# Making the next pair's factors: loads one step ahead and in program order, T1 formed in the chunks, T2 to T4 formed from it on VectorE

## The chip, the cores and the metric

One core of one Trainium2 chip runs the whole program. The metric is the device time of one execution, in microseconds (us).

## The reference, cut to what matters

```
attn = windowed causal attention(q, k, v)        # 4 x 8 heads x 576 x 64, window 128, f32
x    = attn as (2304 tokens, 512)
x2   = (s * relu(x @ moe_w_in)**2 + b) @ moe_w_out        # 512 -> 2048 -> 512
a, b = x2 @ moe2_w1, x2 @ moe2_w2                         # 512 -> 1024 each
out  = ((a * b) @ moe2_w3) @ moe2_w_out                   # 1024 -> 1024 -> 512
```

All of it is float32. The change lies in the last two lines alone.

## The kernel before, in words

The 2304 tokens are six tiles of 384. Attention and the first network run tile by tile and leave x2, transposed, in DRAM (`x2d`), as four blocks of 128 features for each tile. Then `moe2_w3 @ moe2_w_out` is multiplied out once (`w3_unit`, line 601), so that the second network is two matrix products with an elementwise product between them.

These two products run over three **pairs** of token tiles, q = 0, 1, 2. Both are done as a seven-product scheme on two by two blocks (Strassen and Winograd): the blocks B11, B12, B21, B22 of the moving operand are turned into seven **factors**, B11, B21, T1, T2, T4, B22, T3, with T1 = B12 - B11, T2 = B22 - T1, T4 = T2 - B21, T3 = B22 - B12. Every factor is held as a high part (a rounded copy, made by ScalarE) and a low part (the difference, made by a subtraction); `split_to`, lines 652 to 654, does that. A product of two factors is then three passes of matmuls.

A pair has two stages.

**The chunk stage.** `pair_chunk` (line 913) runs for c = 0 to 7. Each chunk has seven products of six matmuls of 128x384 (`prod`, line 886), in the order A11, A12, S1, S2, A22, S4, S3 on TensorE, which is fixed by program order. Four PSUM tiles u, d, e, f take them, in one set of four banks for even chunks and the other for odd ones. ScalarE copies e, u and f out of PSUM (line 901) because the same banks are accumulated on again: S4 adds onto e, so its first matmul waits for the copy of e, which goes into one of two buffers tagged "r" and so waits for the readers of the chunk before. VectorE adds and multiplies (lines 922, 931, 933 to 935), and GpSimd does the last product, p2 (line 936). The results are `prods[c] = (p1, p2)`.

After the fourth product of each chunk but the last, `step` takes one step of `x_later(q + 1)`, which prepares the factors of the next pair: it loads x2 blocks into six buffers tagged "t" (line 796), forms the differences on VectorE (line 815), splits them (line 654) and stores both parts to DRAM (lines 811, 812). In the first pair `step` also takes a step of `w3_factors`, which splits the blocks of the multiplied-out weights with GpSimd for the low parts.

After each odd chunk `w_fetch` (line 754) fetches three weight tiles of 512 KB for the odd chunk two further on. `keep_in_program_order` ties an instruction behind the one that stands before it in the program on the same engine or queue. Instructions without it are placed by a planner that simulates the program's time. In `w_fetch` the three DMAs are tied, in `x_later` only the ScalarE copies are.

**The output stage.** `out_pair` (line 938) takes the eight `prods` as blocks: i = 0 to 3 give B11 and B12, i = 4 to 7 give B21 and B22. `factors` forms and splits the seven factors, four tiles each, into the eight "x" buffers; `product` (line 961) runs 24 matmuls for each, in the order B11 (u), B21 (d), T1 (e), T2 (u), T4 (f), B22 (e), T3 (u). T1, T2 and T4 are formed on VectorE (lines 948, 950, 952), T3 on GpSimd (line 954). `x_fetch` (line 843) fetches the next pair's factors: B11, B21 and T1 before the stage, T2 during it, and T4, B22 and T3 at its end, into the "x" buffers that the output's own factors leave. The results are stored by line 977, some of them from "t" buffers.

All DMAs of this part are issued by one queue, SP's.

Of the kernel before, what the change touches and what calls it, by code (L numbers as in the profile page):

```python
# [8 lines left out]
F32 = mybir.dt.float32  # L9
F32R = mybir.dt.float32r  # L10
# [3 lines left out]
ALU = mybir.AluOpType  # L14
# [13 lines left out]
NC2 = DF2 // P  # L28
# [12 lines left out]
def kernel(  # L41
# [607 lines left out]
        free_w[0] -= 1  # L649
        return wp.tile([P, 2, DM], F32R, tag="w", name="wblk")  # L650

    def split_to(dst, src, eng, pin=lambda i: i, lo_pin=None):
        pin(nc.scalar.activation(out=dst[0], in_=src, func=AF.Copy))  # L653
        (lo_pin or pin)(eng.tensor_tensor(out=dst[1], in0=src, in1=dst[0].bitcast(F32), op=ALU.subtract))  # L654

    wraw, lo_eng = {}, [nc.vector]

# [114 lines left out]
    def x2_at(q, nm, k):  # L772
        return x2d[2 * q + (nm[1] == "2")][k + 2 * (nm[0] == "2")]
# [15 lines left out]
    def x_later(q):  # L789


        def load(k, *nms):
            got[:] = []
            for nm in nms:
                r = lp.tile([P, TT], F32, tag="t", name="xs", bufs=6)
                nc.sync.dma_start(out=r, in_=x2_at(q, nm, k))
                got.append(r)

        def store(k, **rs):
            for nm, r in rs.items():  # L800
                if nz[0] % 3 == 2:
                    z = lp.tile([P, DM], F32, tag="z3", name="xh", bufs=1)[:, :TT]
                else:
                    z = zp.tile([P, TT], F32, tag="z", name="xh")
                nz[0] += 1
                split_to(
                    (z.bitcast(F32R), r.bitcast(F32R)), r, nc.vector,
                    tc.keep_in_program_order, lambda i: i,
                )
                d = xfd[q, nm, k]  # L810
                nc.sync.dma_start(out=d[:, 0, :], in_=z)
                nc.sync.dma_start(out=d[:, 1, :], in_=r)

        def sub(out, a, b):
            nc.vector.tensor_tensor(out=out, in0=a, in1=b, op=ALU.subtract)

        got = []
        load(0, "11", "21")
        yield
        for k in range(2):  # L820
            r11, r21 = got
            store(k, B11=r11, B21=r21)
            load(k, "11", "12", "22", "21")
            yield
            r11, r12, r22, r21 = got
            sub(r12, r12, r11)
            sub(r22, r22, r12)
            sub(r21, r22, r21)
            store(k, T1=r12, T2=r22)
            load(k, "22", "12")  # L830
            yield
            r22, r12 = got
            sub(r12, r22, r12)
            store(k, T4=r21, B22=r22, T3=r12)
            if k == 0:
                load(1, "11", "21")
            yield

    def x_fetch(q, names):
# [70 lines left out]
            t = wp.tile([P, 2 * DM], F32, tag="w", name="p")  # L910
        return [t[:, :TT], t[:, TT:2 * TT]]

    def pair_chunk(c, step):

        tt = nc.vector.tensor_tensor
        pool, tag = (ps_acc, "acc") if c % 2 else (ps_rot, "rot")
        u, d, e, f = (pool.tile([P, TT], F32, tag=tag, name=k) for k in ("u", "d", "e", "f"))
        prods[c] = p1, p2 = p_tiles(c)
        prod(u, "A11", "B11", c, True)
        keep_copy(u, y=p1)  # L920
        prod(d, "A12", "B21", c, True)
        tt(out=p1, in0=d, in1=p1, op=ALU.add)
        prod(e, "S1", "T1", c, True)
        m5 = keep_copy(e, gp, "r")
        prod(u, "S2", "T2", c, False)
        keep_copy(u, y=p2)
        step()
        prod(f, "A22", "T4", c, True)
        m4 = keep_copy(f, gp, "r")
        prod(e, "S4", "B22", c, False)  # L930
        tt(out=p2, in0=e, in1=p2, op=ALU.add)
        prod(u, "S3", "T3", c, False)
        tt(out=m4, in0=u, in1=m4, op=ALU.subtract)
        tt(out=p1, in0=p1, in1=m4, op=ALU.mult)
        tt(out=m5, in0=u, in1=m5, op=ALU.add)  # L935
        nc.gpsimd.tensor_tensor(out=p2, in0=p2, in1=m5, op=ALU.mult)  # L936

    def out_pair(q, before, after):

        tt = nc.vector.tensor_tensor  # L940
        n = NC2 // 2

        def factors(nm):
            ys = []
            for i in range(n):
                (b11, b12), (b21, b22) = prods[i], prods[i + n]
                if nm == "T1":
                    tt(out=b11, in0=b12, in1=b11, op=ALU.subtract)
                elif nm == "T2":
                    tt(out=b11, in0=b22, in1=b11, op=ALU.subtract)  # L950
                elif nm == "T4":
                    tt(out=b21, in0=b11, in1=b21, op=ALU.subtract)
                elif nm == "T3":
                    nc.gpsimd.tensor_tensor(out=b12, in0=b22, in1=b12, op=ALU.subtract)
                src = {"B21": b21, "T4": b21, "B22": b22, "T3": b12}.get(nm, b11)
                y = xp.tile([P, 2, TT], F32R, tag="x", name="pf")
                split_to((y[:, 0, :], y[:, 1, :]), src, nc.vector)
                ys.append(y)
            return ys

        def product(dst, wn, ys, start, outer=False):
            loops = [(i, m) for i in range(n) for m in range(2)]
            if outer:
                loops.sort(key=lambda x: x[1])
            for i, m in loops:
                w, off = w3f[wn, i]
                ms = slice(off + m * P, off + (m + 1) * P)
                for k, (l, r) in enumerate(PASSES):
                    tc.keep_in_program_order(nc.tensor.matmul(  # L969
                        out=dst[m], lhsT=w[:, l, ms], rhs=ys[i][:, r, :],  # L970
                        start=(start and i == 0 and k == 0), stop=(i == n - 1 and k == 2),
                        skip_group_check=True,
                    ))

        def store(z, half, m, t):
            r0 = (2 * half + m) * P
            nc.sync.dma_start(out=out[r0:r0 + P, t * TT:(t + 1) * TT], in_=z)

        d = [ps_rot.tile([P, TT], F32, tag="rot", name="od") for _ in range(2)]
        u = [ps_rot.tile([P, TT], F32, tag="rot", name="ou") for _ in range(2)]  # L980
        e = [ps_acc.tile([P, TT], F32, tag="acc", name="oe") for _ in range(2)]
        f = [ps_acc.tile([P, TT], F32, tag="acc", name="of") for _ in range(2)]
        y = factors("B11")
        before()
        y2 = factors("B21")
        product(u, "A11", y, True)
        m1 = [keep_copy(x, gp, "r") for x in u]
        y = factors("T1")
        product(d, "A12", y2, True)
        for m in range(2):  # L990
            tt(out=m1[m], in0=d[m], in1=m1[m], op=ALU.add)
            store(m1[m], 0, m, 2 * q)
        y2 = factors("T2")
        product(e, "S1", y, True)
        m5 = [keep_copy(x, lp, "t") for x in e]
        y = factors("T4")
        product(u, "S2", y2, False)
        u2 = [keep_copy(x, lp, "t") for x in u]
        y2 = factors("B22")
        product(f, "A22", y, True)  # L1000
        m4 = [keep_copy(x, lp, "t") for x in f]
        y = factors("T3")
        product(e, "S4", y2, False)
        for m in range(2):
            tt(out=u2[m], in0=e[m], in1=u2[m], op=ALU.add)
            store(u2[m], 0, m, 2 * q + 1)
        product(u, "S3", y, False, q == NTILE // 2 - 1)
        after()
        for m in range(2):
            tt(out=m4[m], in0=u[m], in1=m4[m], op=ALU.subtract)  # L1010
            store(m4[m], 1, m, 2 * q)
            tt(out=m5[m], in0=u[m], in1=m5[m], op=ALU.add)
            store(m5[m], 1, m, 2 * q + 1)
        prods.clear()
# [199 lines left out]
    for q in range(NTILE // 2):  # L1214
        more = q + 1 < NTILE // 2
        prep = x_later(q + 1) if more else iter(())
        left = w3_factors() if q == 0 else iter(())

        def step(c):
            if c < NC2 - 1:  # L1220
                next(prep, None)
            next(left, None)
            if c == 0:
                next(left, None)

        for c in range(NC2):
            pair_chunk(c, lambda: step(c))
            if c % 2 and (c + 2 < NC2 or more):
                w_fetch((c + 2) % NC2)
        assert next(prep, None) is None and next(left, None) is None  # L1230

        def fetch(names):
            if more:
                x_fetch(q + 1, names)

        fetch(FACTORS[:3])
        out_pair(q, lambda: fetch(FACTORS[3:4]), lambda: fetch(FACTORS[4:]))
# [69 lines left out]
```

## Time and profile before

| what | value |
|---|---|
| time, median of 3 runs (lowest, highest) | 863.36 us (860.28, 863.45) |
| the profiled execution's own time | 864.42 us |
| its span, first to last instruction | 862.7 us |
| TensorE busy with matmuls | 844.7 us, 98% of the span |
| VectorE, ScalarE, GpSimd busy | 631.0, 522.6, 375.8 us |
| mean granted TensorE clock | 0.998 |

TensorE's busy time counts pipelined matmuls with modelled ends, so what it loses is better read from the times at which stages begin than from the busy share. Engines are called PE (TensorE), DVE (VectorE), ACT (ScalarE), POOL (GpSimd) and SP (the queue that issues the DMAs).

### The profile page before, as it was taken

How to read it: one execution, taken by the hardware profiler on the slowest of the kernel's cores; microseconds unless marked ns; L12 is line 12 of the kernel's file. 1: busy time of each engine (PE TensorE's matmuls, PEld its weight loads, DVE VectorE, ACT ScalarE, POOL GpSimd, SP SyncE). 2: the span in 40 equal slices, each digit the busy share in tenths (PEclk: the TensorE clock that was granted, in tenths of full speed). 3: DMA queues.
4: the chain of work that ended last, by engine and by line, in shares of the span. 5: the costliest groups of instructions: out<-in, count | busy, mean ns of one | idle time of the engine just before them, and what ended most of it. 6: DMA issues, size and time to landing. Idle time of an engine off the chain costs nothing.

```text
span 862.7 us, 14152 instructions
## 1 busy us (share of the span) xinstructions
PE 844.7 (98%) x4746; PEld 782.3 (91%) x4748; DVE 631.0 (73%) x1276; ACT 522.6 (61%) x1240; POOL 375.8 (44%) x383
## 2 busy tenths in 40 slices
PE   9999999999999999999999999999999998999998
PEld 5766667999999999999999999879998898899997
DVE  5889987777878788788863987867488455853385
ACT  6777769787877777777765665434446233442244
POOL 0234458788667767666651200855340011301130
PEclk9999999999999999999999999999999999999999
DMA  9856512113355555445324498972882867646001
GB/s 336 318 183 216 184 55 92 55 56 104 97 177 174 168 173 177 153 156 187 110 98 149 148 349 328 351 277 80 261 298 84 285 226 272 243 165 220 1 10 64
DMA packets 58968, 152.72 MB, mean 177 GB/s; under 512 B 6800, under 2 KB 25488, under 8 KB 58896
## 3 DMA queue, kind: packets, MB, share of 16 engines
q1 hardware_dynamic: 58896, 151.83, 50.9%
q8 instruction: 37, 0.61, 0.3%
q14 instruction: 35, 0.29, 0.1%
HBM read 113.00 MB, written 38.80 MB: 176 GB/s over the span
## 4 chain that ended last, share of the span: by engine, by line
PE 81%; DVE 7%; DMA 5%; ACT 3%; issue 3%; POOL 1%; SPq 0%; DVEq 0%; ACTq 0%; POOLq 0%
PE hp L514 19%; PE acc L566 19%; PE u L892 7%; PE e L892 5%; PE acc L560 4%; PE hp L505 4%; PE pv L440 4%; PE ou L969 3%; PE oe L969 3%; PE d L892 2%; DVE pf L654 2%; PE f L892 2%; PE s L310 2%; PE s L311 2%; PE of L969 1%
## 5 line engine op out<-in xcount | busy, mean ns | idle before, releaser
L514 PE MATMUL hp<-x,w 128*128 128x384 f32 x960 | 185.1, 339 | 0.0
L514 PEld LDWEIGHTS hp<-x,w 128*128 128x128 f32 x960 | 167.3, 188 | 0.3
L566 PE MATMUL acc<-gh,w 128*128 128x384 f32 x640 | 125.9, 338 | 0.0
L566 PEld LDWEIGHTS acc<-gh,w 128*128 128x128 f32 x640 | 109.1, 188 | 0.2
L936 POOL TENSOR_TENSOR p<-p,mc 128x384 f32<-128x384 f32 x24 | 29.2, 1217 | 174.7 <-DVE mc L935 155.4
L403 POOL TENSOR_SCALAR_AFFINE_SELECT pt<-pp 128x768 fp32r<-128x768 f32 x80 | 78.9, 1009 | 30.9 <-PE pv L440 16.7
L892 PE MATMUL u<-xb,wblk 128*128 128x384 f32 x432 | 84.8, 338 | 1.6 <-DMA xb<-xfd_T 1.6
L272 POOL TENSOR_TENSOR kb<-qkraw,ka 128x512 fp32r<-128x512 f32 x40 | 57.1, 1426 | 56.2 <-ACT ka L271 55.8
L892 PEld LDWEIGHTS u<-xb,wblk 128*128 128x128 f32 x432 | 76.5, 190 | 2.5 <-DMA xb<-xfd_T 1.6
L324 DVE CUSTOM_DVE_ANT_0 ns<-s,relm_sb 128x256 f32<-128x256 f32 (+1 forms) x144 | 53.2, 412 | 30.4 <-PE s L311 22.9
L368 POOL TENSOR_SCALAR pr<-pr,sm 128x128 f32<-128x128 f32 x90 | 45.7, 522 | 65.4 <-ACT z L150 22.3
L566 PE MATMUL acc<-gl,w 128*128 128x384 f32 x320 | 69.6, 337 | 0.0
L543 DVE TENSOR_TENSOR gl<-r,gh 128x384 fp32r<-128x384 f32 x80 | 57.0, 713 | 14.5 <-ACT gh L535 13.3
L901 ACT ACTIVATE p<-u 128x384 f32<-128x384 f32 x48 | 23.6, 491 | 69.3 <-PE u L892 69.3
L525 ACT ACTIVATE r<-hp 128x384 f32<-128x384 f32 x96 | 46.5, 484 | 29.4 <-PE hp L514 27.9
L892 PE MATMUL e<-xb,wblk 128*128 128x384 f32 x288 | 58.1, 336 | 4.7 <-ACT mc L901 4.7
L347 ACT ACTIVATE pr<-pr,mn 128x128 f32<-128x128 f32 x120 | 46.9, 392 | 20.3 <-DVE pr L333 20.0
L654 DVE TENSOR_TENSOR pf<-p,pf 128x384 fp32r<-128x384 f32 x84 | 49.1, 615 | 13.1 <-ACT pf L653 12.6
L566 PEld LDWEIGHTS acc<-gl,w 128*128 128x128 f32 x320 | 56.6, 188 | 0.0
L892 PEld LDWEIGHTS e<-xb,wblk 128*128 128x128 f32 x288 | 50.4, 188 | 6.0 <-ACT mc L901 6.0
L653 ACT ACTIVATE pf<-p 128x384 fp32r<-128x384 f32 x84 | 40.2, 518 | 21.4 <-DVE p L950 9.6
L530 ACT ACTIVATE r<-r 128x384 f32<-128x384 f32 x96 | 49.8, 519 | 1.6
(144 smaller groups left out, 1871.2 us busy)
## 6 DMA issues: line engine op xcount, KB each, us to landing
qkraw<-qk SPq DMA_DIRECT2D x40, 448.0 KB, 3.3
late<-st SPq DMA_DIRECT2D x23, 512.0 KB, 3.4
w<-late SPq DMA_DIRECT2D x23, 512.0 KB, 6.8
wblk<-wfd_S SPq DMA_DIRECT2D x22, 512.0 KB, 7.0
raw<-w_in SPq DMA_DIRECT2D x16, 512.0 KB, 6.6
raw<-w_out SPq DMA_DIRECT2D x16, 512.0 KB, 6.4
wr<-w SPq DMA_DIRECT2D x16, 512.0 KB, 5.1
st<-w3T SPq DMA_DIRECT2D x15, 512.0 KB, 3.6
```

Of the source, the lines that this page charges most:

```text
L272: nc.gpsimd.tensor_tensor(out=kl, in0=k_r, in1=k.bitcast(F32), op=ALU.subtract)
L324: nc.vector.tensor_tensor_reduce(out=n[:, i, cs], in0=dst[i][:, cs], in1=relm_sb[:, VARIANT.get(t * NB + i, 0), cs], scale=2.0 ** -(h + 1) ...
L347: nc.scalar.activation(out=e[:, i, :], in_=e[:, i, :], func=AF.Exp, scale=-1.0, bias=mn[:, i:i + 1], accum_out=sm[:, i:i + 1],)
L403: nc.gpsimd.affine_select(out=o[:, :, :, e, :], in_=pp.bitcast(F32), pattern=[[0, 2], [0, NB], [sign, P]], compare_op=op, fill=0.0, base=0 ...
L514: nc.tensor.matmul(out=hp, lhsT=wi[c][:, l, k * P:(k + 1) * P], rhs=xT[t, k][:, r, :], start=(n == 0), stop=(n == 3 * KD - 1),)
L525: chain(t * NC1 + c, nc.scalar.activation(out=rt[:, :TT], in_=hps.pop((t, c)), func=AF.Relu))
L530: chain(t * NC1 + c, nc.scalar.activation(out=rt[:, :TT], in_=rt[:, :TT], func=AF.Square))
L543: nc.vector.tensor_tensor(out=gl, in0=rt[:, :TT], in1=gh.bitcast(F32), op=ALU.subtract)
L566: nc.tensor.matmul(out=x2acc[m], lhsT=wo[c][:, l, ms], rhs=g[r], start=(c == 0 and n == 0), stop=(c == NC1 - 1 and n == 2),)
L654: (lo_pin or pin)(eng.tensor_tensor(out=dst[1], in0=src, in1=dst[0].bitcast(F32), op=ALU.subtract))
L892: tc.keep_in_program_order(nc.tensor.matmul(out=dst, lhsT=w[:, l, ks], rhs=xblk[bnm, k][:, r, :], start=(start and n == 0), stop=(n == 5), ...
L969: tc.keep_in_program_order(nc.tensor.matmul(out=dst[m], lhsT=w[:, l, ms], rhs=ys[i][:, r, :], start=(start and i == 0 and k == 0), stop=(i ...
```

## The change

In `x_later` each step first issues the loads of the next step and then works on those of the step before, and the loads, the differences and both halves of each split are all tied to program order; the stores are not. T1 of the output stage is formed inside chunks 1 to 4, into the p2 tile. In the output stage T2, T4 and T3 are formed from it by VectorE (T3 as T2 - B11, which is the same value), and GpSimd does nothing there. The last product of a chunk, p2, goes to VectorE for every chunk of the second and third pair and for the last chunk of the first; GpSimd keeps seven of the first pair.

```diff
--- before.py
+++ after.py
@@ -649,9 +649,9 @@
         free_w[0] -= 1
         return wp.tile([P, 2, DM], F32R, tag="w", name="wblk")
 
-    def split_to(dst, src, eng, pin=lambda i: i, lo_pin=None):
+    def split_to(dst, src, eng, pin=lambda i: i):
         pin(nc.scalar.activation(out=dst[0], in_=src, func=AF.Copy))
-        (lo_pin or pin)(eng.tensor_tensor(out=dst[1], in0=src, in1=dst[0].bitcast(F32), op=ALU.subtract))
+        pin(eng.tensor_tensor(out=dst[1], in0=src, in1=dst[0].bitcast(F32), op=ALU.subtract))
 
     wraw, lo_eng = {}, [nc.vector]
 
@@ -789,12 +789,15 @@
     def x_later(q):
 
 
+        pin = tc.keep_in_program_order
+
         def load(k, *nms):
-            got[:] = []
+            rs = []
             for nm in nms:
                 r = lp.tile([P, TT], F32, tag="t", name="xs", bufs=6)
-                nc.sync.dma_start(out=r, in_=x2_at(q, nm, k))
-                got.append(r)
+                pin(nc.sync.dma_start(out=r, in_=x2_at(q, nm, k)))
+                rs.append(r)
+            return rs
 
         def store(k, **rs):
             for nm, r in rs.items():
@@ -803,37 +806,31 @@
                 else:
                     z = zp.tile([P, TT], F32, tag="z", name="xh")
                 nz[0] += 1
-                split_to(
-                    (z.bitcast(F32R), r.bitcast(F32R)), r, nc.vector,
-                    tc.keep_in_program_order, lambda i: i,
-                )
+                split_to((z.bitcast(F32R), r.bitcast(F32R)), r, nc.vector, pin)
                 d = xfd[q, nm, k]
                 nc.sync.dma_start(out=d[:, 0, :], in_=z)
                 nc.sync.dma_start(out=d[:, 1, :], in_=r)
 
         def sub(out, a, b):
-            nc.vector.tensor_tensor(out=out, in0=a, in1=b, op=ALU.subtract)
-
-        got = []
-        load(0, "11", "21")
+            pin(nc.vector.tensor_tensor(out=out, in0=a, in1=b, op=ALU.subtract))
+
+        ahead = load(0, "11", "21")
         yield
         for k in range(2):
-            r11, r21 = got
+            (r11, r21), ahead = ahead, load(k, "11", "12", "22", "21")
             store(k, B11=r11, B21=r21)
-            load(k, "11", "12", "22", "21")
             yield
-            r11, r12, r22, r21 = got
+            (r11, r12, r22, r21), ahead = ahead, load(k, "22", "12")
             sub(r12, r12, r11)
             sub(r22, r22, r12)
             sub(r21, r22, r21)
             store(k, T1=r12, T2=r22)
-            load(k, "22", "12")
             yield
-            r22, r12 = got
+            r22, r12 = ahead
+            if k == 0:
+                ahead = load(1, "11", "21")
             sub(r12, r22, r12)
             store(k, T4=r21, B22=r22, T3=r12)
-            if k == 0:
-                load(1, "11", "21")
             yield
 
     def x_fetch(q, names):
@@ -910,7 +907,7 @@
             t = wp.tile([P, 2 * DM], F32, tag="w", name="p")
         return [t[:, :TT], t[:, TT:2 * TT]]
 
-    def pair_chunk(c, step):
+    def pair_chunk(c, step, mul):
 
         tt = nc.vector.tensor_tensor
         pool, tag = (ps_acc, "acc") if c % 2 else (ps_rot, "rot")
@@ -920,6 +917,9 @@
         keep_copy(u, y=p1)
         prod(d, "A12", "B21", c, True)
         tt(out=p1, in0=d, in1=p1, op=ALU.add)
+        if 0 < c <= NC2 // 2:
+            b11, b12 = prods[c - 1]
+            tt(out=b12, in0=b12, in1=b11, op=ALU.subtract)
         prod(e, "S1", "T1", c, True)
         m5 = keep_copy(e, gp, "r")
         prod(u, "S2", "T2", c, False)
@@ -933,7 +933,7 @@
         tt(out=m4, in0=u, in1=m4, op=ALU.subtract)
         tt(out=p1, in0=p1, in1=m4, op=ALU.mult)
         tt(out=m5, in0=u, in1=m5, op=ALU.add)
-        nc.gpsimd.tensor_tensor(out=p2, in0=p2, in1=m5, op=ALU.mult)
+        mul.tensor_tensor(out=p2, in0=p2, in1=m5, op=ALU.mult)
 
     def out_pair(q, before, after):
 
@@ -944,15 +944,13 @@
             ys = []
             for i in range(n):
                 (b11, b12), (b21, b22) = prods[i], prods[i + n]
-                if nm == "T1":
+                if nm == "T2":
+                    tt(out=b12, in0=b22, in1=b12, op=ALU.subtract)
+                elif nm == "T4":
+                    tt(out=b21, in0=b12, in1=b21, op=ALU.subtract)
+                elif nm == "T3":
                     tt(out=b11, in0=b12, in1=b11, op=ALU.subtract)
-                elif nm == "T2":
-                    tt(out=b11, in0=b22, in1=b11, op=ALU.subtract)
-                elif nm == "T4":
-                    tt(out=b21, in0=b11, in1=b21, op=ALU.subtract)
-                elif nm == "T3":
-                    nc.gpsimd.tensor_tensor(out=b12, in0=b22, in1=b12, op=ALU.subtract)
-                src = {"B21": b21, "T4": b21, "B22": b22, "T3": b12}.get(nm, b11)
+                src = {"B21": b21, "T4": b21, "B22": b22, "T1": b12, "T2": b12}.get(nm, b11)
                 y = xp.tile([P, 2, TT], F32R, tag="x", name="pf")
                 split_to((y[:, 0, :], y[:, 1, :]), src, nc.vector)
                 ys.append(y)
@@ -1224,7 +1222,7 @@
                 next(left, None)
 
         for c in range(NC2):
-            pair_chunk(c, lambda: step(c))
+            pair_chunk(c, lambda: step(c), nc.vector if q or c == NC2 - 1 else nc.gpsimd)
             if c % 2 and (c + 2 < NC2 or more):
                 w_fetch((c + 2) % NC2)
         assert next(prep, None) is None and next(left, None) is None
```

## Rows read from the trace of the kernel before

**Rows 1.** Stretches: length, busy PE, PEld, DVE, ACT, POOL, clock, DMA share, GB/s.

```profile
579.99:641.48 61.49, 59.12 (x337) 58.19 (x336) 40.31 (x76) 28.96 (x64) 26.94 (x22) 1.00 0.58 188
641.48:673.20 31.72, 30.70 (x169) 28.92 (x169) 24.81 (x46) 14.85 (x32) 4.69 (x4) 1.00 0.44 164
673.20:738.10 64.90, 60.91 (x337) 59.73 (x337) 33.56 (x66) 22.52 (x50) 9.62 (x8) 0.97 0.79 268
738.10:769.65 31.55, 30.48 (x169) 28.97 (x169) 24.64 (x46) 14.86 (x32) 5.24 (x4) 1.00 0.40 149
769.65:827.89 58.24, 58.24 (x337) 58.24 (x337) 22.91 (x44) 17.87 (x38) 9.63 (x8) 1.00 0.35 125
827.89:858.73 30.84, 30.24 (x169) 28.87 (x168) 24.28 (x47) 13.49 (x31) 4.79 (x4) 1.00 0.09 34
683.00:684.00 1.00, 1.00 (x5) 1.00 (x4) 0.87 (x2) 0.00 (x0) 0.00 (x0) 0.50 0.77 212
```

**Rows 2.** Waits of TensorE over the whole span: total us, times, longest.

```profile
PE e L892 <- ACT mc L901: 4.7, 4, 2.2
PE od L969 <- ACT pf L653: 1.7, 3, 0.7
PE u L892 <- DMA xb<-xfd_T: 1.6, 2, 1.3
PE w3a L601 <- DMA w<-late: 1.5, 2, 1.2
...
PE od L969 <- DVE pf L654: 1.0, 5, 0.3
```

**Rows 3.** TensorE in order of time: start, duration, [idle before <- releaser].

```profile
623.37 1.33 PE L892 MATMUL e<-xb,wblk 128*128 128x384 f32 x6 [1.34 <-ACT mc L901]
...
656.03 4.85 PE L969 MATMUL ou<-pf,w3f 128*128 128x384 f32 x24
...
681.63 3.32 PE L892 MATMUL u<-xb,wblk 128*128 128x384 f32 x11 [1.30 <-DMA xb<-xfd_T]
684.75 1.68 PE L892 MATMUL d<-xb,wblk 128*128 128x384 f32 x6
...
720.89 1.31 PE L892 MATMUL e<-xb,wblk 128*128 128x384 f32 x6 [2.21 <-ACT mc L901]
```

**Rows 4.** VectorE in order of time, same columns.

```profile
626.40 0.56 DVE L815 TENSOR_TENSOR xs<-xs 128x384 f32<-128x384 f32 x1 [3.20 <-DMA xs<-x2d]
...
642.25 0.54 DVE L948 TENSOR_TENSOR p<-p 128x384 f32<-128x384 f32 x1
...
643.19 1.36 DVE L948 TENSOR_TENSOR p<-p 128x384 f32<-128x384 f32 x1
...
648.26 1.37 DVE L934 TENSOR_TENSOR p<-p,mc 128x384 f32<-128x384 f32 x1
```

**Rows 5.** GpSimd in order of time, same columns.

```profile
642.94 1.20 POOL L954 TENSOR_TENSOR p<-p 128x384 f32<-128x384 f32 x1 [1.49 <-DVE p L948]
```

**Rows 6.** SP's queue in order of time: when DMAs were issued.

```profile
595.02 1.88 SPq L812 DMA_DIRECT2D xfd_B<-xs  x2
...
605.31 0.38 SPq L754 DMA_DIRECT2D wblk<-wfd_A  x1
...
674.15 0.32 SPq L796 DMA_DIRECT2D xs<-x2d  x1
...
675.52 0.37 SPq L843 DMA_DIRECT2D xb<-xfd_T  x1
...
768.84 1.36 SPq L843 DMA_DIRECT2D xb<-xfd_T  x2
```

**Rows 7.** DMA issues by kind: size, median us from issue to landing.

```profile
wblk<-wfd_S SPq DMA_DIRECT2D x22, 512.0 KB, 7.0
...
xs<-x2d SPq DMA_DIRECT2D x32, 192.0 KB, 3.2
...
wblk<-wfd_A SPq DMA_DIRECT2D x11, 512.0 KB, 5.4
```

## The prediction

> **What bounds the kernel now.** I read three views: the busy time by stretch, to find where TensorE loses time; its list of waits, to see whom it waits for; and the engines in order of time around each wait. TensorE is the bound, busy for 844.7 of 862.7 us (the table above). Only the three pairs are touched, so the first view is cut at their stages, and there the third pair's chunk stage is the yardstick: 58.24 us for 336 matmuls, TensorE busy for all of it [rows 1]. That is 0.1733 us a matmul, 1.04 for a product of six, 7.28 for a chunk; an output stage of 168 matmuls should take 29.12 (29.28 for the last, with the last matmul's end). Against that the stages lose
>
> - first pair: 61.49 - 58.24 = 3.25 and 31.72 - 29.12 = 2.60
> - second pair: 64.90 - 58.24 = 6.66 and 31.55 - 29.12 = 2.43
> - third pair: 0 and 30.84 - 29.28 = 1.56,
>
> 16.5 us together [rows 1]. More than that the change can't give in these stages.
>
> The waits name three causes. First, S4's product waits 4.7 us in four places for ScalarE's copy of e [rows 2]. ScalarE is only the messenger: it waits for VectorE to read the "r" buffer, and VectorE stands in a difference of `x_later` whose operand has not landed: idle 3.20 us before line 815 at 626.40 [rows 4], and what is queued behind it is late for the next chunk. TensorE stops so before 623.37 and 720.89 [rows 3], and shorter two more times. Second, the second pair's T3 waits 1.6 us for its fetch [rows 2]. Third, the output's second product, od, waits 1.7 + 1.0 us for its factors [rows 2], and T2's takes 4.85 us where 24 matmuls need 4.16 and a tail of 0.16 [rows 3].
>
> **The change, part by part.**
>
> *Loads a step ahead.* Each difference now uses data asked for one chunk, 7.28 us, before; a load lands in 3.2 [rows 7]. Six buffers hold two old and four new tiles, so a load waits only for stores of the step before, which leaves about 4 us. The loss this can recover is the first pair's 3.25 and, in the second, what the T3 fetch leaves (below): 6.66 - 3.71 = 2.95. Of these 6.2 I take 5.2: 4.7 is the wait itself, and each of the four restarts shows a first product of 1.3 instead of 1.2 us [rows 3]. Bounds 0 and 6.2.
>
> *The tie of the loads also moves other DMAs.* The second pair's first two loads wait for a "t" buffer, which a store of the output holds. One was issued at 674.15, and the second T3 fetch behind them only at 675.52 [rows 6]; it was needed at 673.20 + 6 x 1.04 = 679.44. In the third pair, which has no `x_later`, the same two fetches went out from 768.84, 0.8 us before the stage, and nobody waited [rows 6, 1]. With the tie the loads come behind the output's last store, so the second pair should look like the third. Here the wait costs more than itself: after the idle 1.30 the eleven matmuls take 3.32 us and the next six 1.68 (6 take 1.20 elsewhere) [rows 3], at a granted clock of 0.50, the lower of its two levels, 1.2 GHz [rows 1]. Its d product ends at 684.75 + 1.68 - 0.16 = 686.27, due at 673.20 + 7.28 + 2.08 = 682.56: 3.71 lost. After the idle 2.21 before 720.89 the product took 1.31, no halving [rows 3]. I take all 3.7; bounds 0 and 3.7.
>
> *The weight fetches move later.* This is the price. `w_fetch` is tied behind the DMA before it in the program. That was a load; now, with the order in the step reversed, it is the step's last low-part store, which waits for ScalarE's copy and VectorE's difference. Chunk 5's fetch of the first pair went out at 605.31 [rows 6], 11.1 us ahead of that chunk's start at 579.99 + 5 x 7.28 = 616.39. Now it stands as late as a store: step 1's last two took from 595.02 to 596.90 [rows 6], 9.6 us after their chunk's start at 587.27, when the chunk that needs the weights is 14.56 after it. The first tile lands 5.4 later, at 15.0: 0.4 late; the next (0.4 us of issue later, 7.0 to land, needed 2.08 later) at 17.0 against 16.64: 0.4 late too. That chunk had GpSimd's weight splits beside it; elsewhere a copy after the fourth product (4.2 us), two or three copies and differences of 0.55 and the issues give some 8 us, which is in time. Six fetches (chunks 3, 5, 7 of two pairs): I take 0.2 each, 1.2; nothing below, 2.7 to 3.8 each above (rivals).
>
> Here a rule of the Trainium skill speaks against the change. DMA: Bandwidth & Descriptors, section "Queues, rings and completion order", says that each DMA engine takes the descriptors of one ring in order; a fetch issued behind four or six stores would then stand behind all their bytes. By that the sum would be +3.9 us instead of -13.3 if none of those bytes had left before; no row isolates it.
>
> *The output stage.* Removed: T1's four differences on VectorE, and T3's four on GpSimd. GpSimd's matter through VectorE: the same difference takes 0.54 us alone (642.25) and 1.36 (643.19) while GpSimd's at 642.94 runs [rows 4, 5]. So VectorE reaches chunk 7's p1 product only at 648.26 [rows 4], 6.8 us after that chunk ended, and od's last factor is made from it. Afterwards VectorE has before that factor four low parts of B11, three of B21 and five operations of chunk 7: 12 x 0.55 = 6.6 us. They can begin when T2's buffers are free, 641.48 - 3 x 1.04 = 638.36, and a copy of some 0.5 is made; begun at 638.9 they are done at 645.5; copy and low part make 646.6. The need is 641.48 + 4.16 + 3.12 = 648.76: 2.2 spare, about four operations. Added: T3's four on VectorE, 2.2 us per pair, needed last; the stage has VectorE busy 24.8 of 31.7 [rows 1], and T1's leave. If that cover were gone, 6.6 over three pairs. Of the 2.60 + 2.43 + 1.56 = 6.6 lost I take 5.6, leaving 0.3 a pair; bounds 0 and 6.6.
>
> *VectorE in the chunks.* T1 costs 4 x 0.55 = 2.2 us a pair, the p2 product 4.4 in pairs two and three and 0.55 in the first, and up to eight differences of `x_later` (4.4) may move into the first pair's stage. VectorE then has 40.3 + 7.2 = 47.5 of 58.2, 33.6 + 6.6 = 40.2 and 22.9 + 6.6 = 29.5 [rows 1]: nothing, while what waits in its queue is short. The waits for late weights before the pairs, 1.5 us [rows 2], I leave as they are.
>
> **Sum.** -5.2 - 3.7 - 5.6 + 1.2 = -13.3 us. The profiled execution took 864.42, its span 862.7 with 1.7 around it; 864.42 - 13.3 = 851.1. It is 1.06 above the median, so 850.1 for the median.
>
> **Rivals** (by the median).
>
> - *Weights late, in part*: 1.2 us a fetch, half the break-even below: -14.5 + 7.2 = -7.3, 856.1. For it, the margins above lie within 2 us; against it, the 0.4 was worked out for the most crowded of the six steps. 15%.
> - *Slower: weights late in full.* Every fetch stands behind the bytes of its step's stores: four or six of 192 KB, 0.79 or 1.18 MB, at 268 / 0.79 = 339 GB/s [rows 1] 2.3 or 3.4 us. With the 0.4 above, 4 x 2.7 + 2 x 3.8 = 18.4: 864.42 - 14.5 + 18.4 = 868.3, median 867.2. It decides against the change from 14.5 / 6 = 2.4 us a fetch; a halved clock as at 681.63 would help it. Against it: the first stores leave while the last wait, and the 5.4 and 7.0 were measured among other DMAs. The ring order of the Trainium skill's page is this mechanism. 5%.
> - *Loads still late* (now behind fetches and stores on SP): the 5.2 stay, 855.3. 10%.
> - *The output's order stays bad* in VectorE's queue: 5.6 stay, 855.7. 8%.
> - *T3's fetch stays late*, held up by something else: 3.7 stay, 853.8. 7%.
>
> **Numbers.** The forecast case has 55%, between 847 and 853.5. With two rivals at once, 88% for faster by over 0.5% (4.3 us, about what a measurement of this kernel can tell from no change), 7% within, 5% slower. The range 846.5 to 857 leaves out the fully late weights, pairs of rivals, and little below: all 16.5 gone would be 846.9.
>
> **What would show it.** No wait before e and none for T3, with the clock at 1.00 throughout the second pair; its chunk stage near 58.5; the outputs near 29.5, chunk 7's p1 product within 4 us of its end, GpSimd idle in them. Wrong would be: waits of A11's or S1's product for a weight fetch in chunks 3, 5, 7, or line 815's successor idle for a load.

## The result, and the profile after

The changed kernel takes 854.52 us (median of 6 runs, 854.22 to 856.53), the kernel before 863.34 beside it: ratio 0.9907, 95% interval 0.9889 to 0.9926. That is 8.8 us faster, inside the range of 846.5 to 857, and 4.4 us short of the 850.1 that was forecast. Some executions, whatever the version, run longer at a lower clock; the ratios leave the slowest of them out, and the run with the second pair's loads untied, which is one, is read by its stage alone.

The busy time by stretch, cut at the stages as in [rows 1], shows that the pairs gave more than was forecast, and a stretch ahead of them lost. The columns are those of [rows 1].

```profile
585.14:644.98 59.84, 58.57 (x338) 58.25 (x337) 48.14 (x84) 29.17 (x64) 26.57 (x21) 1.00 0.66 223
644.98:674.10 29.12, 29.12 (x170) 29.12 (x170) 22.16 (x46) 15.42 (x32) 0.00 (x0) 1.00 0.48 180
674.10:732.34 58.24, 58.24 (x338) 58.24 (x338) 38.85 (x78) 22.38 (x50) 0.00 (x0) 1.00 0.87 295
732.34:761.46 29.12, 29.12 (x170) 29.12 (x170) 22.16 (x46) 15.42 (x32) 0.00 (x0) 1.00 0.45 164
761.46:819.70 58.24, 58.24 (x338) 58.24 (x338) 27.83 (x56) 17.86 (x38) 0.00 (x0) 1.00 0.35 125
819.70:848.98 29.28, 29.28 (x169) 28.96 (x168) 22.49 (x47) 13.59 (x31) 0.00 (x0) 1.00 0.10 35
567.60:572.50 4.90, 0.04 (x1) 0.00 (x0) 2.49 (x3) 1.38 (x3) 2.37 (x3) 1.00 1.01 374
572.50:574.00 1.50, 1.49 (x4) 1.22 (x5) 0.00 (x0) 0.00 (x0) 0.70 (x1) 0.55 1.00 391
574.00:576.00 2.00, 2.00 (x7) 1.54 (x6) 0.00 (x0) 0.00 (x0) 0.00 (x0) 0.50 1.03 422
```

The first pair's chunk stage fell from 61.49 to 59.84, the second's from 64.90 to 58.24, and the output stages to 29.12, 29.12 and 29.28, the times at which TensorE never waits. From the start of the pairs to the end of the last output the kernel takes 848.98 - 585.14 = 263.84 us, before 858.73 - 579.99 = 278.74: 14.9 us less. But the pairs start 5.15 us later (585.14 for 579.99). The last three rows show where: TensorE does nothing from 567.6 to 572.5, in the product of the two weight matrices (`w3_unit`), and then runs at a granted clock of 0.55 and 0.50, the lower level, until 576. Its waits (total, times, longest, as in [rows 2]) say for whom.

```profile
PE w3a L601 <- DMA w<-late: 4.9, 1, 4.9
...
PE e L889 <- ACT mc L898: 1.3, 1, 1.3
```

These late weights (tiles that `w3_unit` reads, loaded by line 1174, `w<-late`) were waited for 1.5 us before [rows 2], and now 4.9. The waits for T3 and of od are gone from the list, and of the 4.7 us before e, 1.3 is left. (Line numbers differ between versions: `prod` is line 892 before and 889 here.) SP's queue, in order of time, shows what changed in front of the late weights; first the kernel before, then the changed one.

```profile
552.41 6.19 SPq L796 DMA_DIRECT2D xs<-x2d  x5
562.84 0.33 SPq L84 DMA_DIRECT2D raw<-w3T  x1
563.22 1.59 SPq L1176 DMA_DIRECT2D w<-late  x3
```

```profile
563.39 0.33 SPq L84 DMA_DIRECT2D raw<-w3T  x1
563.78 2.81 SPq L798 DMA_DIRECT2D xs<-x2d  x6
566.63 2.03 SPq L1174 DMA_DIRECT2D w<-late  x3
```

Before, five of the first pair's loads went out while the queue was going to wait anyway, for the raw load at 562.84 (`raw<-w3T`, a weight block that is decoded on the chip), and the three late weights followed at 563.22. Now all six stand between the raw load and the weights, which go out at 566.63, 3.4 us later. From there to TensorE's start it is 5.9 us (566.63 to 572.51), before 5.2 (563.22 to 568.40), so most of the delay is the later issue and some 0.7 us a slower landing.

### The profile page after: what moved, and what is told of

The parts are those of the page before. It is cut to its first block, busy times and chain, and to the rows that moved or that the text cites. A ratio compares the mean times of both kernels' runs of the same rounds, so it can differ in the third digit from the quotient of the medians.

```text
span 853.3 us, 14121 instructions
## 1 busy us (share of the span) xinstructions
PE 838.6 (98%) x4746; PEld 782.2 (92%) x4748; DVE 639.2 (75%) x1305; ACT 524.0 (61%) x1240; POOL 342.5 (40%) x354
## 4 chain that ended last, share of the span: by engine, by line
PE 88%; DVE 3%; ACT 3%; DMA 2%; POOL 1%; issue 1%; SPq 1%; DVEq 0%; ACTq 0%; POOLq 0%
PE hp L514 20%; PE acc L566 20%; PE u L889 8%; PE e L889 6%; PE ou L967 4%; PE acc L560 4%; PE hp L505 4%; PE pv L440 4%; PE oe L967 3%; PE f L889 3%; PE d L889 3%; PE w3a L601 2%; PE s L310 2%; PE s L311 2%; PE of L967 1%; PE od L967 1%
## 5 line engine op out<-in xcount | busy, mean ns | idle before, releaser
L654 DVE TENSOR_TENSOR pf<-p,pf 128x384 fp32r<-128x384 f32 x84 | 44.1, 552 | 15.1 <-ACT pf L653 14.4
L601 PE MATMUL w3a<-w 128*128 128x512 f32 x192 | 46.0, 400 | 4.9 <-DMA w<-late 4.9
```

The source lines that it names most:

```text
L601: nc.tensor.matmul(out=accs[i], lhsT=w3g[i // 4, j][:, l, i % 4 * P:(i % 4 + 1) * P], rhs=wo2s[j][:, r, :], start=(j == 0 and n == 0), sto ...
```

## The experiments

Eleven runs follow. Two versions, the first six loads untied and the same with p2 on VectorE in every pair, have intervals wholly below that of the changed kernel, each measured against the kernel before on its own chip. Four versions were executed once and are read by stages and waits; the others also by time.

**The first six loads untied.**

```diff
-        def load(k, *nms):
+        def load(k, *nms, tied=True):
...
-                pin(nc.sync.dma_start(out=r, in_=x2_at(q, nm, k)))
+                i = nc.sync.dma_start(out=r, in_=x2_at(q, nm, k))
+                if tied:
+                    pin(i)
...
-        ahead = load(0, "11", "21")
+        ahead = load(0, "11", "21", tied=q != 1)
...
-            (r11, r21), ahead = ahead, load(k, "11", "12", "22", "21")
+            (r11, r21), ahead = ahead, load(k, "11", "12", "22", "21", tied=q != 1 or k > 0)
```

> The changed kernel with the first six loads of the first pair not tied to program order; all else as changed. Theory 1 (the six tied loads stand on SP in one block ahead of the three late weight loads of the stage before the pairs): the three go out some 3 us earlier, the wait of w3a for a late weight falls from 4.9 to about 1.5 us in all, the granted clock stays at 1.00 behind it, and the time falls by 3.4 + 1.3 = 4.7 us, to about 849.8. Rival (those weights are late for the load ahead of them, which waits for GpSimd, or for DMA traffic): no change, 854.5, wait still near 4.9.

849.66 us, ratio to the kernel before 0.9854 (0.9831 to 0.9877). Its wait for late weights, and SP's queue:

```profile
PE w3a L601 <- DMA w<-late: 1.6, 1, 1.6
```

```profile
552.30 6.20 SPq L798 DMA_DIRECT2D xs<-x2d  x5
562.73 0.33 SPq L84 DMA_DIRECT2D raw<-w3T  x1
563.12 1.56 SPq L1176 DMA_DIRECT2D w<-late  x3
```

The weights are back at 563.12 and the wait at 1.6. The 48 matmuls behind it take 11.53 us instead of 12.79 in the changed kernel. Theory 1 holds, with the number that it gave.

**The first six loads behind the weights.**

```diff
+                kept[0] = nc.sync.dma_start(out=wfd[c, names], ...)
...
+        if q == 1:
+            with tc.issue_after(kept[0].ins):
+                ahead = load(0, "11", "21")
+        else:
+            ahead = load(0, "11", "21")
```

> The changed kernel with the first six loads put behind the last store of split weights, so behind all the late weight loads on SP. Theory 1: as in the run with the loads untied, 849.8, and down to 848.3 if the six loads also were what kept the 1.5 us of before; the loads still land by about 575, some 20 us before their first reader, so no new wait in chunks 1 and 2. Rival: 854.5, wait still near 4.9; or a new wait of chunk 1 for the loads.

Ratio 0.9882 (0.9840 to 0.9924); the profiled execution took 849.6 us, span 847.9. The three weights go out at 563.32, the six loads from 569.33, and w3a waits 1.5 us, with no new wait in the chunks. So the place of the loads is what counts, and that TensorE waited 1.5 us before the change was not their doing. The time alone doesn't show it: the interval of the ratio reaches over the changed kernel's 0.9907.

**One part at a time.** First the output part alone, with `x_later` and `split_to` as before; then the loads part alone, with `pair_chunk` and `out_pair` as before.

> The kernel before with the output part of the change alone: T1 in the chunks, T2 to T4 from it on VectorE, p2 on VectorE in pairs two and three. If the parts add: the output stages fall to 29.1, 29.1 and 29.3 us, 6.6 less, time 856.7; the waits before e (4.7) and for T3 with the halved clock (3.7) stay, the late weights cost 1.5 as before. Rival (VectorE's added work lengthens its queue, so that the late loads cost more than before): e waits over 4.7, time 857 to 860.

> The kernel before with the loads part alone: loads a step ahead, tied. If the parts add: chunk stages near 59.8, 58.2, 58.2, output stages as before (31.7, 31.6, 30.8), late weights 4.9 as in the changed kernel, time 854.5 + 6.6 = 861.1. Rival (part of the chunk gain comes from GpSimd's p2 and port use): chunk stages of 59 to 61 in pair two, time up to 863.

The busy time by stretch of the output part alone (first pair's chunk and output stage, second pair's), and its waits:

```profile
579.43:642.15 62.72, 59.17 (x338) 58.09 (x336) 45.22 (x81) 28.87 (x64) 25.78 (x21) 1.00 0.56 185
642.15:671.27 29.12, 29.12 (x170) 29.12 (x169) 22.17 (x46) 15.42 (x32) 0.00 (x0) 1.00 0.49 176
671.27:736.61 65.34, 60.71 (x338) 59.76 (x337) 37.48 (x78) 22.35 (x50) 0.00 (x0) 0.97 0.82 270
736.61:765.73 29.12, 29.12 (x170) 29.12 (x169) 22.17 (x46) 15.42 (x32) 0.00 (x0) 1.00 0.43 157
```

```profile
PE e L892 <- ACT mc L901: 4.9, 2, 2.8
PE u L892 <- DMA xb<-xfd_T: 1.8, 2, 1.4
PE u L892 <- ACT p L901: 1.4, 1, 1.4
```

The output stages are at 29.12 by this part alone, as the theory said. But the chunk stages grow, to 62.72 and 65.34 (61.49 and 64.90 in [rows 1]): 1.2 and 0.4 us more, and there is a new wait of 1.4 for ScalarE's copy of u into p. That is the rival's direction, a longer queue on VectorE behind a late load; which operation caused it was not followed up. In time the part is not told from no change (ratio 0.9988, 0.9955 to 1.002); its profiled execution has a span of 857.3, where 862.7 - 6.6 + 1.7 = 857.8 is what the stages give.

The loads part alone, the same four stages:

```profile
585.26:644.76 59.50, 58.69 (x337) 58.20 (x336) 44.71 (x79) 29.07 (x64) 27.48 (x22) 1.00 0.65 223
644.76:676.50 31.74, 30.73 (x170) 28.95 (x169) 24.82 (x46) 14.88 (x32) 4.68 (x4) 1.00 0.44 165
676.50:734.74 58.24, 58.24 (x338) 58.24 (x337) 33.92 (x68) 22.41 (x50) 9.41 (x8) 1.00 0.87 298
734.74:766.02 31.28, 30.48 (x169) 28.94 (x169) 24.36 (x45) 14.90 (x32) 5.14 (x5) 1.00 0.41 149
```

Its chunk stages, 59.50 and 58.24, are near those of the changed kernel (59.84 and 58.24), its output stages within 0.3 us of those of before, and w3a waits 4.8 us: 861.49 us, ratio 0.9987 (0.9964 to 1.001), against 861.1 expected. Alone, this part takes 8.9 us from the four stages (1.99 + 6.66 from the chunk stages, the rest from the output) and gives back 5.3 in front of the pairs, which start at 585.26 for 579.99; the 3.6 that are left are about the span's 3.2 (859.5 for 862.7), and the times are not told apart. Of the waits before e one is left, in the first pair's chunk 3:

```profile
PE e L889 <- ACT mc L898: 0.8, 1, 0.8
```

**The second pair's loads untied**, the same edit as in the first run with `q != 2`.

> The changed kernel with the first six loads that the second pair makes for the third not tied to program order. Theory 1 (the second pair's T3 fetch was late because these loads stood before it on SP, waiting for a buffer that an output store held): the wait of T3's product for its fetch comes back, 1.6 to 1.8 us, perhaps with the halved clock behind it, and the second pair's chunk stage grows from 58.2 to 60.0 to 62.0 us. Rival (the fetch was helped by the output stage without GpSimd): no wait, 58.2.

The second pair's chunk stage, 681.47 to 744.17, takes 62.70 us instead of 58.24. The wait, SP's queue and TensorE:

```profile
PE u L891 <- DMA xb<-xfd_T: 2.3, 2, 1.3
```

```profile
682.28 0.32 SPq L798 DMA_DIRECT2D xs<-x2d  x1
682.70 0.37 SPq L842 DMA_DIRECT2D xb<-xfd_T  x1
683.17 0.38 SPq L798 DMA_DIRECT2D xs<-x2d  x1
683.65 0.37 SPq L842 DMA_DIRECT2D xb<-xfd_T  x1
```

```profile
689.21 0.41 PE L891 MATMUL u<-xb,wblk 128*128 128x384 f32 x1 [1.34 <-DMA xb<-xfd_T]
690.63 3.75 PE L891 MATMUL u<-xb,wblk 128*128 128x384 f32 x11 [1.01 <-DMA xb<-xfd_T]
```

The two T3 fetches again stand each behind a load, 2.3 us of waits come back, and the eleven matmuls take 3.75 us: the granted clock was 0.51 from 690.6 to 692.5. In the changed kernel both fetches go out from 673.28, 0.8 us before the stage begins at 674.10, and the six loads only after the output's last stores, at 677.32:

```profile
673.28 1.36 SPq L840 DMA_DIRECT2D xb<-xfd_T  x2
```

The output stage is as in the changed kernel, so the tie is what helped T3.

**Every store of the factors doubled**, the second copy to DRAM that nothing reads.

```diff
                 nc.sync.dma_start(out=d[:, 1, :], in_=r)
+                d = dp.tile([P, 2, TT], F32, name=f"xfe_{q}_{nm}_{k}")
+                nc.sync.dma_start(out=d[:, 0, :], in_=z)
+                nc.sync.dma_start(out=d[:, 1, :], in_=r)
```

> The changed kernel with every store of the next pair's factors issued a second time, to DRAM that nobody reads, so that each weight fetch stands behind 8 or 12 stores instead of 4 or 6. The margins that the first tiles of the six fetches have in the changed kernel are 3.4, 1.3, 0.3 and 3.7, 2.2, 2.1 us. Theory 1 (only the issue on SP, about 0.4 us each, moves the fetch; bytes ahead of it have mostly left): fetches issued 1.6 to 2.4 us later, about 2.5 us of waits for weights in all. Rival (a fetch lands behind all the bytes issued before it, 339 GB/s): 2.3 to 3.4 us later still, some 13 us of waits, with the clock halved behind some.

The waits, and SP's queue at the three fetches of the first pair:

```profile
PE u L892 <- DMA wblk<-wfd_A: 5.5, 2, 3.1
...
PE u L892 <- ACT p L901: 1.9, 2, 1.0
PE u L892 <- DVE p L937: 1.8, 1, 1.8
```

```profile
601.24 0.46 SPq L754 DMA_DIRECT2D wblk<-wfd_A  x1
...
620.20 0.32 SPq L754 DMA_DIRECT2D wblk<-wfd_A  x1
...
636.52 0.46 SPq L754 DMA_DIRECT2D wblk<-wfd_A  x1
```

Neither forecast fits in size. Weights are waited for 5.5 us, at chunk 7 of the first pair and chunk 5 of the second. Another 1.9 go to ScalarE's copies, and 1.8, before chunk 5 of the first pair, are put down to VectorE's product into p1 (line 937); but they ended at 624.00, when that chunk's first weight tile landed too (620.20 + 3.7 = 623.9), so they can't be told from a wait for weights. In the first pair the fetches of chunks 3 and 5 leave 2.0 and 2.8 us later after the stage's start than in the changed kernel (601.24 for 599.58, 620.20 for 617.73, with the pairs begun 0.3 earlier). From issue the three of a step land about as soon as there: 3.6 to 5.3 us for chunk 3 and 3.7 to 5.7 for chunk 5, where the changed kernel has 4.0 to 5.6 and 3.9 to 5.9. The two fetches that are on the waits' list leave 4.7 and 4.8 us later and land somewhat slower: 5.8 to 6.9 for 5.0 to 6.4, and 4.8 to 7.6 for 4.2 to 6.3. So most of what moved the fetches is their issue; 0.5 to 1.3 us at these two may be the bytes ahead of them, less than the rival's 2.3 to 3.4.

**p2 on GpSimd everywhere**, `mul` always GpSimd.

> The changed kernel with the p2 product on GpSimd in every chunk of every pair, as before. Theory 1 (what freed the output stage is that VectorE has neither T1's differences nor GpSimd's T3 beside it; p2's place hardly counts): stages as in the changed kernel, the three output stages 29.1 to 29.6, time within 0.7 of 854.5. Rival (p2 on GpSimd delays the next chunk's copy of e, or the factors of the last chunk): waits before e or od, 1 us or more a pair.

855.02 us, and every stage of the pairs is that of the changed kernel within 0.01 us (59.83, 29.12, 58.24, 29.12, 58.24, 29.29). Where p2 is made in the second and third pair, and in the last chunk, counts for nothing. Which of the other two edits of the output part freed its stages, T1 moved into the chunks or T3 taken from GpSimd, no run separates.

**Loads ahead, nothing tied** but ScalarE's copies, as before the change.

> The changed kernel with the loads a step ahead but not tied, nor the differences and low parts. Theory 1 (each tie acts through SP's order: bad before the pairs, good for the second pair's T3 fetch): late weights cost 1.5 us as before, T3's fetch is late again (chunk stage of pair two 60 to 63 us), the differences no longer wait for loads, so the other chunk stages lie near 58.2 to 59.8. Rival (the ties of the differences are what keeps VectorE's queue short): waits before e of 2 us or more.

852.16 us, span 850.4, and no halved clock (the second pair's chunk stage at 1.00). Its waits:

```profile
PE w3a L601 <- DMA w<-late: 1.7, 2, 1.4
PE u L889 <- DMA xb<-xfd_T: 1.4, 1, 1.4
...
PE e L889 <- ACT mc L898: 0.6, 1, 0.6
```

The chunk stages take 58.58 and 60.84 us. This version differs from the output part alone by the order of the loads in the program, one step earlier, and that takes the waits before e from 4.9 to 0.6 (the 0.6 lies in the second pair). Against this version the ties cost 3.9 us before the pairs (585.14 for 581.23, though here the stages ahead ran 0.6 later) and 1.3 in the first pair's chunk stage (59.84 for 58.58), and gain 2.6 in the second's (58.24 for 60.84), where T3's fetch is late here.

**Untied, and p2 on VectorE in the first pair too.** The 1.3 us left before e in the changed kernel lie in the first pair's chunk 3. VectorE there, some us before:

```profile
602.39 1.63 DVE L922 TENSOR_TENSOR p<-p 128x384 f32<-128x384 f32 x1 [0.91 <-POOL p L936]
603.94 1.65 DVE L815 TENSOR_TENSOR xs<-xs 128x384 f32<-128x384 f32 x1
```

T1's difference waits 0.91 for p2 on GpSimd, and GpSimd then splits five weight blocks for 6.45 us beside VectorE, some of whose operations take up to 1.65 where they take 0.55 alone.

> The version with the first six loads untied, and p2 on VectorE also in the first pair. The 1.3 us wait before e in chunk 3 of the first pair is what the pairs still lose. Theory 1 (T1's difference on VectorE waits for p2 on GpSimd there, and what is queued behind it with it): the wait goes, time 848.3 against 849.7. Rival (VectorE is slow there because GpSimd splits five weight blocks beside it): the wait stays or grows by up to seven more products of 0.55, 849.7 to 852.

> The version with the first six loads untied and p2 on VectorE everywhere, again, for its time and an undisturbed profile: no wait before e in the first pair, whose chunk stage is 58.3 to 58.6 us; time 848.3, ratio about 0.983.

In the first run the ratio is 0.9833 (0.9815 to 0.9851), in the second 0.9833 (0.9802 to 0.9863), the lowest times 848.16 and 847.87. The chunk stages of the first two pairs in the second run:

```profile
582.34:640.61 58.27, 58.27 (x338) 58.26 (x336) 47.56 (x91) 29.31 (x64) 18.35 (x14) 1.00 0.67 229
669.73:727.97 58.24, 58.24 (x338) 58.24 (x337) 38.97 (x78) 22.40 (x50) 0.00 (x0) 1.00 0.86 294
```

No wait before e is left, and the first pair's stage is 0.03 over 58.24. That doesn't show that the difference's wait was the cause, because GpSimd's splits moved too: without p2 they begin at 596.36, 14.0 us after the stage's start, where in the changed kernel they begin at 602.32, 17.2 after it. Two earlier runs speak against that cause alone. In the loads part alone no T1 difference stands in the chunks, and 0.8 of the 1.3 us is there all the same. With nothing tied, p2 on GpSimd and its five splits (6.46 us) are as in the changed kernel, the difference waits as long,

```profile
598.48 1.63 DVE L922 TENSOR_TENSOR p<-p 128x384 f32<-128x384 f32 x1 [0.91 <-POOL p L936]
```

and the first pair has no wait before e. ScalarE's copy of e in chunk 3 tells what each piece is worth: from the stage's start it begins at 27.96 us in the changed kernel, at 27.49 in the loads part alone, at 26.55 with nothing tied and at 26.12 here. So T1's difference, with its wait, is worth about 0.5 by these runs; the order that the ties give VectorE's queue, beside GpSimd's splits, is worth 1.4, both measured at the copy; of that lateness TensorE waited for 1.3 us. One execution of each shows this, and how the two act together was not tested further.

This version has the lowest ratio; against the first run (0.9854, on another chip) its time is not told apart, its stage is.

**The late weights ahead of the raw load.** The last version, with the loads behind the weights and

```diff
-        raw_load(raw, src)
+        with tc.issue_after(lasts[-2].ins):
+            raw_load(raw, src)
```

> As the version before, but with the six loads behind the last store of split weights, and with the three late weight loads ahead on SP of the raw load that waits for GpSimd. Theory 1 (the three only stand behind that raw load): the 1.5 us wait of w3a goes, time 846.8. Rival: the raw load, now behind them, lands late, and its weight, decoded by four engines' work, holds up the last of w3a's units by 2 to 6 us: 850 to 854.

Ratio 0.9852 (0.9812 to 0.9892). The waits:

```profile
PE w3a L601 <- ACT w L125: 1.8, 1, 1.8
```

The wait for the late loads is gone, but the raw load goes out some 4 us later, 29.1 us after the stores of the last x2 blocks begin (24.8 in the version before), and the weight decoded from it is 1.8 us late. Nothing is won: it is the rival's mechanism, with a wait just below its 2 to 6 us.

## Why the prediction was right, and where it fell short

The direction and the range held, and the terms in the pairs came out within 1.2 us each. Step by step, the term first and then what it measured:

- *Loads a step ahead*: 5.2 taken, 3.25 - 1.60 = 1.65 in the first pair and all 2.95 in the second, 4.6. What is left in the first pair is the queue on VectorE in chunk 3: tied differences and splits that take up to 1.65 us beside GpSimd's splits, and T1's difference that waits 0.91 for p2. It goes without the ties or with p2 on VectorE; how it divides rests on one execution each (about 0.5 for T1's difference). I had counted VectorE's work in the chunks as nothing "while what waits in its queue is short", at 0.55 us an operation; its busy time was right (48.1 us for 47.5), the queue was not short.
- *T3's fetch*: 3.7 taken, 3.7 gained (the second pair's 6.66 is all gone; its division into 3.71 and 2.95 is that of the trace before). Untying the second pair's loads alone brings the wait and the halved clock back, 4.46 us in that stage. The part of it that the clock costs is not there in every execution: with the output part alone T3 waits 1.8 us and the clock behind it stays at 1.00.
- *Weight fetches*: 1.2 taken, nothing lost. Chunk 3's fetch of the first pair went out at 599.58, 7.2 us after the start of chunk 1, not 9.6, and its three tiles landed in 4.0 to 5.6 us, not 5.4 to 7.0:

```profile
599.58 0.45 SPq L754 DMA_DIRECT2D wblk<-wfd_A  x1
```

  The two rivals on them did not come; with the stores doubled the fetches are late, mostly through their issue.
- *Output stage*: 5.6 taken, 2.60 + 2.43 + 1.56 = 6.6 gained, by the output part alone too. Chunk 7's p1 product runs on VectorE soon after its chunk:

```profile
646.65 0.55 DVE L934 TENSOR_TENSOR p<-p,mc 128x384 f32<-128x384 f32 x1
```

  1.7 us after the chunk's end at 644.98, before 6.8 [rows 4].
- *The late weights before the pairs*: their 1.5 us, "I leave as they are". This is the step that failed. It measured 5.15: 0.44 in which the stages before already ran later, 3.37 of longer waiting (4.87 for 1.50) and the rest, 1.3, at the halved clock. I asked of the second pair's loads which DMA the tie puts them behind, and not of the first pair's. There the DMA before them in the program is the raw load, which is not tied itself and goes out early; the six loads follow it and stand before the three late weights, as SP's queue shows. Two ways of moving them away bring the wait back to 1.6 and 1.5 us, and the first of them between 4.6 us (by the ratios) and 4.9 us (by the medians) of time.

Sum: -14.9 in the pairs, +5.15 before them, +0.35 at the end (from the last matmul 4.32 us for 3.97): -9.4, which is the span's 862.7 - 853.3. With the wait left at about 1.5, as in the first run, the kernel takes 849.7; 850.1 was forecast. That this is so close is in part luck: the fetches and the output stage came out 1.2 and 1.0 us better than forecast, the loads 0.6 worse, and the forecast was also moved by 1.06 from the profiled execution to the median.

DMA: Bandwidth & Descriptors in the Trainium skill, section "Queues, rings and completion order", says that on each DMA engine descriptors are taken in ring order. Read as in the prediction, that a fetch stands behind all the bytes issued before it, it would have made the change slower by 3.9 us. The trace does not agree with that price: with twice the bytes ahead of them, two fetches of the first pair landed as soon as without, and the two that were waited for 0.5 to 1.3 us later, in one execution.

## What to carry to other kernels

An instruction tied to the one before it in the program is tied to whatever stands there, and if that one floats, the tie carries it to where it floats: look up the predecessor of each tied DMA, and who waits behind the block, in every place where the code runs. Here, issuing loads one step earlier took most of the waits away without any tie, so a tie is worth adding where a run shows a queue in the wrong order. When a wait goes after an edit, see what else the edit moved before naming its cause: p2's move also moved GpSimd's splits, and a run made for another purpose showed the same 0.91 us of waiting without harm.

## What the runs showed of the hardware that I had not expected

The granted clock of TensorE fell to the lower of its two levels after some waits and not after others of like length. It was at 0.50 to 0.55 behind an idle of 4.87 us (changed kernel), and at 0.51 behind 1.34 and 1.01 with one matmul between (second pair's loads untied), as before behind 0.31 and 1.30. But behind 0.41 and 1.41 at the same place (output part alone) it stayed at 1.00, as it did behind one idle of 1.40 (nothing tied) and behind 2.21 [rows 3]; behind 2.81 (output part alone) it fell to 0.50. So a wait before T3 cost its own length, or up to 2.1 us more, and these traces don't tell beforehand which.

VectorE was slowed beside GpSimd in some operations only. While GpSimd split blocks from 602.32 to 608.77 in the changed kernel, VectorE's differences of two SBUF tiles took up to 1.65 us, but the add at 605.51, which reads d from PSUM, took 0.55.
